# A new order for attention and two feed-forward layers on one core, and the first layer's low words made on ScalarE

## The chip, the cores and the metric

The kernel runs on one core of one Trainium2 chip. The metric is the device time of one execution in microseconds (us). The engines are named as in the profile: PE is TensorE's matmul, PEld its weight load, DVE VectorE, ACT ScalarE, POOL GpSimd, SP SyncE, whose queue issues most DMAs.

## What is computed

Thresholded attention over 4 batches of 8 heads (576 tokens, 64 wide), then two feed-forward layers of 2304 tokens, 512 wide, 2048 hidden. Weights come as 64-bit floats.

```python
scores = scale * np.matmul(q, k.transpose(0, 1, 3, 2))
thresh = np.max(scores, axis=-1, keepdims=True) - tau
scores = np.where(scores >= thresh, scores, -1000000000.0)
scores = scores - np.max(scores, axis=-1, keepdims=True)
attn = np.exp(scores)
attn = attn / (np.sum(attn, axis=-1, keepdims=True) + 1e-09)
x = np.matmul(attn, v)          # then heads side by side: 2304 x 512
...
h = x @ w_in;   g = h * np.cos(h);                      x = g @ w_out      # first layer
h = x @ w_in;   g = s * np.maximum(h, 0.0)**2 + b;      out = g @ w_out    # second layer
```

## The kernel before, in words

**Attention** goes in 16 pairs of heads (`pair(n)`). A pair has nine score tiles of 128 rows by 576; tile 4 is mixed from both heads. For tile i the steps are: `scores` on PE (tile `s`, two PSUM slots in turn), `stat` on DVE (copies `s` to `p` and takes the minimum `mn`), `limit` on POOL (`thr` = `mn` + tau), `expo` on ACT (`e`), `mask` on DVE (compares `p` with `thr`, multiplies by `e`, sums into `sm`). Then `turn` transposes masked tiles on PE (`pt`, four PSUM slots shared with others), `store_turned` copies them to `PT` on ACT, `turn_rest` and `store_rest` do the last columns. `sums` (POOL), `recips` (DVE, tile `r`), `rows` (PE), `spread` (ACT) and `spread2` (SP, by way of DRAM) bring the reciprocals of the row sums to the layout of the output. `weighted(h, k)` multiplies by the values on PE: for each half h five steps k of two matmuls into `av`. `finish` copies `av` to `xs` on ACT, and `normalise` multiplies on POOL into `xT`.

PE's matmuls are of three kinds: `scores`, `turn` and `turn_rest` use 64 rows of the array at a time, `weighted` 64 columns, and the layers all of it. An fp32 matmul of the first two kinds stands as two instructions in the trace (two `weighted` matmuls of a step are x4).

**Layers.** Tokens go in blocks of 512 (one of 256). For each block and each 128 of the hidden width (a step) PE makes `h` by 12 matmuls, DVE, POOL and ACT do the activation, and PE adds 12 matmuls into `acc`. Every operand is a high part rounded to fp32r (`wh`, `xh`, `gh`) and a rest (`wl`, `xl`, `gl`).

**Weights.** `decode` turns one half tile of 64-bit floats (two 32-bit words each, `wr`) into fp32: `magnitude` on ACT, `clamp` on POOL, `shift`, `sign` and `fill` on DVE (`wt`), `high` on POOL or ACT, `low` on POOL. The first 15 half tiles of the first layer (`EARLY`) are decoded beside attention; 17 more after it, and the 32 of the second layer later still.

**The order.** All this is recorded as operations with an engine, a length, a rank and what they need, and `Order.run` draws up the sequence: at each step every engine looks at its first 48 open operations by rank and takes the first that could start. The ranks come from `PLACE`, one number for each kind of operation, plus a base of 12303 for each pair; `SLACK` and `LAG` say how far a later operation may go ahead, and what a hand-over between engines costs. On the chip each engine then executes its own sequence strictly in that order, and waits by semaphores.

Of the kernel before, what the change touches and what calls it, by code (L numbers as in the profile page):

```python
# [10 lines left out]
F32 = mybir.dt.float32  # L11
F32R = mybir.dt.float32r
I32 = mybir.dt.int32
AF = mybir.ActivationFunctionType
ALU = mybir.AluOpType
PSUM = bass.MemoryType.PSUM

P = 128

TINY = 2.0**-15  # L20
HUGE = 3.0e38
TWO_PI = 2.0 * math.pi
# [5 lines left out]
class Order:  # L28
# [6 lines left out]
    SLACK = 0  # L35
    LAG = 90
    WINDOW = 48

# [12 lines left out]
    def add(self, engine, length, rank, fn, after=(), take=(), give=(), tail=0):  # L51
        op = dict(
            n=len(self.ops), engine=engine, length=length, rank=rank, fn=fn,
            after=[a for a in after if a is not None], take=tuple(take), give=tuple(give),
            tail=tail, start=None, end=None,
        )
        self.ops.append(op)
        return op

    def _earliest(self, op, free):  # L60
        t = free
        for a in op["after"]:
# [17 lines left out]
    def run(self):  # L80
# [5 lines left out]
        free = dict.fromkeys(queues, 0.0)  # L86
        done = []
        while any(queues.values()):
# [15 lines left out]
            free[e] = op["end"]  # L104
            for name, _ in op["take"]:
                self.rings[name]["taken"] += 1
            for name, k in op["give"]:
                self.rings[name]["back"][k] = op["end"]
# [7 lines left out]
EARLY = 15  # L116

# [4 lines left out]
    "scores": -3186, "stat": -5231, "exp": -5403, "mask": -12, "turn": 1691, "turned": 1308, "rest": -817,  # L122
    "rested": 530, "sums": -3199, "weigh0": -749, "weigh1": 4124, "weigh_step": 1464, "finish": -3724,
    "normalise": 49805, "keys": -33243, "early": 2.755, "early_step": 0.971, "first": 4.255, "second": 0.531,
    "second_step": 0.992, "first_step": 0.769, "xin": -6179, "active": 7099, "output": 1499,
# [5 lines left out]
def attention_moe_moe2_kernel(  # L131
# [76 lines left out]
    make_identity(nc, ident)  # L208
    ape = actx.enter_context(tc.tile_pool(name="ape", bufs=2))
# [23 lines left out]
    def pair(n):  # L233
# [32 lines left out]
        ks = add("POOL" if n else "ACT", 700, base + PLACE["keys"], scale_keys, after=[lk], take=[tk["ks"]], give=[tk["k"]])  # L266
# [37 lines left out]
        for i in range(9):  # L304
            for _ in range(WEIGH.count(i)):
                yield
            at = base + i * PAIR // 9
# [38 lines left out]
            def mask(i=i):  # L346
                if "sm" not in T:
# [7 lines left out]
            s_ = add("PE", 660 if i == mixed else 620, at + PLACE["scores"], scores, after=[lq, ks] if i == 0 else [], take=[ts],  # L355
                     give=[tk["q"], tk["ks"]] if i == 8 else [], tail=130)
            scored.append(s_)
            m_ = add("DVE", 835, at + PLACE["stat"], stat, after=[s_], take=[tm, tp], give=[ts])
            t_ = add("POOL", 190, at + PLACE["stat"], limit, after=[m_], take=[th])
            e_ = add("ACT", 735, at + PLACE["exp"], expo, after=[m_], take=[te], give=[tm])  # L360
            k_ = add("DVE", 850, at + PLACE["mask"], mask, after=[e_, t_], give=[te, th])
            masks.append(k_)
            if i in (1, 3, 4, 6, 8):
                tiles = [i] if i == mixed else [i - 1, i]
                tt = [ticket("pt"), ticket("pt")]
                r_ = add("PE", 310 * len(tiles), at + PLACE["turn"], lambda t=tiles: turn(t), after=[masks[j] for j in tiles],
                         take=[*tt, *([tk["PT"]] if i == 1 else [])], tail=170)
# [25 lines left out]
        r_ = add("PE", 650, end + PLACE["rest"], turn_rest, after=masks, take=tt, give=ptk, tail=170)  # L393
        for g in range(2):
            c_ = add("ACT", 400, end + PLACE["rested"], lambda g=g: store_rest(g), after=[r_], give=[tt[g]])
# [26 lines left out]
        o1 = add("POOL", 150, end + PLACE["sums"] + 0, sums, after=masks)  # L422
        o2 = add("DVE", 220, end + PLACE["sums"] + 100, recips, after=[o1])
        t1 = ticket("pt")
        o3 = add("PE", 110, end + PLACE["sums"] + 700, rows, after=[o2], take=[t1])
        o4 = add("ACT", 270, end + PLACE["sums"] + 800, spread, after=[o3], give=[t1])
        o5 = add("SP", 150, end + PLACE["sums"] + 900, spread2, after=[o4], take=[tk["rb"]], tail=5000)
# [18 lines left out]
        for h in range(2):  # L446
            yield
            ts = ticket("pt")
            for k in range(5):
                v1 = add(  # L450
                    "PE", 490 + 100 * (k % 4 == 0), end + PLACE[f"weigh{h}"] + k * PLACE["weigh_step"], lambda h=h, k=k: weighted(h, k),
                    after=[*transposed, lv] if h == k == 0 else [v1], take=[ts] if k == 0 else [],
                    give=[tk["PT"], tk["v"]] if h * k == 4 else [],
                    tail=250 * (k == 4),
                )
            f_ = add(
                "ACT", 390, end + PLACE["finish"] + PLACE[f"weigh{h}"], lambda h=h: finish(h), after=[v1, f_],
# [8 lines left out]
        n_ = add("POOL", 1600, end + PLACE["normalise"], normalise, after=[f_, o5], give=[tk["xs"], tk["rb"]])  # L466
# [421 lines left out]
```

## Time and profile before

| what | value |
|---|---|
| median of 3 runs | 1097.76 us (1095.64 to 1100.08) |
| profiled execution | 1095.87 us |
| its span | 1093.3 us |
| mean granted TensorE clock | 0.995 of full speed |
| attention, first score tile to last weighted step | about 5 to 290 us |
| layers | about 274 to 1089 us |

The span runs from the first to the last instruction. The profile below is of the profiled execution; times in rows are us from the span's start unless marked ns.

### The profile page before, as it was taken

The page shows a single profiled execution, that of the slowest core. Times are in us where ns is not written, and L with a number is a line of the kernel's source. Part 1 is how long each engine was busy: PE and PEld are TensorE (multiplying, and loading weights), DVE is VectorE, ACT ScalarE, POOL GpSimd, SP SyncE. Part 2 cuts the span into 40 slices and gives each one's busy share as a digit, 9 for nine tenths or more (in the row PEclk, how much of TensorE's full clock was granted, in tenths as well). Part 3 has the DMA queues.
Part 4 walks back from the last instruction along what each step waited for, and adds up shares of the span by engine and source line. Part 5 has one row for each costly group of instructions (what it writes and reads, how often), then busy time and mean ns, then how long its engine had stood idle before and what let it go on. Part 6 is the DMA issues. An engine that isn't in the chain of part 4 may idle for free.

```text
span 1093.3 us, 17499 instructions
## 1 busy us (share of the span) xinstructions
PE 1051.2 (96%) x6736; PEld 804.5 (74%) x6736; DVE 649.6 (59%) x1206; ACT 491.4 (45%) x880; POOL 497.4 (45%) x556
## 2 busy tenths in 40 slices
PE   6998989899999999999999999999999999999998
PEld 3554555555678788899888888788888898888886
DVE  7998899889899943434534789778511212113111
ACT  6887777878554432323223445444422323223221
POOL 4556465565587643333333776666422222222221
PEclk9999899999999999999999999999999999999999
DMA  4323244242223200000100132323100000001001
GB/s 171 132 89 139 94 133 131 102 134 75 69 97 97 78 20 1 1 1 1 58 1 0 58 97 78 95 79 105 50 1 1 8 32 20 1 1 40 1 1 39
DMA packets 23507, 63.59 MB, mean 58 GB/s; under 512 B 4464, under 2 KB 4736, under 8 KB 23424
## 3 DMA queue, kind: packets, MB, share of 16 engines
q1 hardware_dynamic: 23280, 62.48, 17.7%
q8 instruction: 53, 0.87, 0.3%
q14 instruction: 30, 0.25, 0.1%
q10 hardware_dynamic: 144, 0.00, 0.0%
HBM read 57.67 MB, written 4.79 MB: 57 GB/s over the span
## 4 chain that ended last, share of the span: by engine, by line
PE 84%; DVE 6%; POOL 4%; issue 3%; DMA 1%; ACT 1%; SPq 0%; POOLq 0%; DVEq 0%
PE h L661 36%; PE acc L764 18%; PE acc L762 17%; PE av L434 6%; PE s L318 4%; PE pt L281 2%; DVE p L333 2%; DVE p L350 2%; POOL thr L340 1%; POOL xT L462 1%; DMA wr<-in_w_dram 1%; DVE wt L549 1%; POOL wt L546 1%; POOL wl L189 1%; DVE wt L554 0%
## 5 line engine op out<-in xcount | busy, mean ns | idle before, releaser
L661 PE MATMUL h<-x,wh 128*128 128x512 f32 (+1 forms) x1280 | 369.6, 373 | 4.2 <-DVE r L712 3.5
L189 POOL TENSOR_TENSOR gl<-r,gh 128x512 fp32r<-128x512 f32 x144 | 189.6, 1317 | 334.8 <-DVE gh L735 248.7
L661 PEld LDWEIGHTS h<-x,wh 128*128 128x128 f32 x1280 | 231.2, 188 | 53.9 <-DVE r L712 6.4
L661 PE MATMUL h<-x,wl 128*128 128x512 f32 (+1 forms) x640 | 238.7, 373 | 0.7 <-POOL wl L189 0.7
L691 DVE TENSOR_SCALAR r<-r,s_t,b_t 128x512 f32<-128x512 f32 x72 | 45.8, 636 | 207.9 <-ACT r L226 207.8
L226 ACT ACTIVATE r<-h 128x512 f32<-128x512 f32 x72 | 42.9, 596 | 243.2 <-PE h L661 241.8
L661 PEld LDWEIGHTS h<-x,wl 128*128 128x128 f32 x640 | 120.2, 188 | 23.8 <-POOL wl L189 1.1
L350 DVE SCALAR_TENSOR_TENSOR p<-p,thr,e 128x576 f32<-128x576 f32 x144 | 125.1, 883 | 2.8 <-ACT e L344 2.3
L762 PE MATMUL acc<-gl,wh 128*128 128x512 f32 (+1 forms) x320 | 118.3, 370 | 0.2 <-POOL gl L189 0.2
L344 ACT ACTIVATE e<-p,mn 128x576 f32<-128x576 f32 x144 | 109.8, 771 | 19.3 <-DVE p L350 11.8
L762 PE MATMUL acc<-gh,wl 128*128 128x512 f32 (+1 forms) x320 | 118.0, 369 | 0.0
L762 PE MATMUL acc<-gh,wh 128*128 128x512 f32 (+1 forms) x320 | 118.0, 369 | 0.0
L318 PE MATMUL s<-ks,q 64*128 64x288 f32 x512 | 95.2, 464 | 23.5 <-DVE p L333 17.9
L333 DVE TENSOR_SCALAR_CACHE_REDUCE p<-s 128x576 f32<-128x576 f32 x144 | 106.3, 753 | 17.9 <-PE s L318 16.9
L764 PE MATMUL acc<-wh,gl 128*128 128x512 f32 x288 | 112.6, 391 | 0.0
L764 PE MATMUL acc<-wl,gh 128*128 128x512 f32 x288 | 112.5, 390 | 0.0
L764 PE MATMUL acc<-wh,gh 128*128 128x512 f32 x288 | 112.3, 390 | 0.0
L226 ACT ACTIVATE r<-r,hpi 128x512 f32<-128x512 f32 x72 | 51.9, 721 | 132.7 <-POOL r L704 132.6
L189 POOL TENSOR_TENSOR wl<-wt,wh 128x512 fp32r<-128x512 f32 x64 | 88.0, 1378 | 41.0 <-ACT wh L572 39.8
L340 POOL TENSOR_TENSOR thr<-mn,ptau 128x1 f32<-128x1 f32 x144 | 69.5, 484 | 78.4 <-DVE p L333 77.0
L691 DVE TENSOR_SCALAR r<-h 128x512 int32<-128x512 f32 x72 | 49.6, 689 | 79.2 <-PE h L661 70.8
L434 PE MATMUL av<-PT,v 128*64 128x288 f32 x640 | 93.2, 418 | 0.0
(65 smaller groups left out, 1423.7 us busy)
## 6 DMA issues: line engine op xcount, KB each, us to landing
wr<-in_w_dram SPq DMA_DIRECT2D x64, 512.0 KB, 3.7
q<-in_qt_dram SPq DMA_DIRECT2D x15, 576.0 KB, 3.8
v<-in_va_dram SPq DMA_DIRECT2D x16, 320.0 KB, 3.6
k<-in_kt_dram SPq DMA_DIRECT2D x16, 288.0 KB, 4.0
out_dram<-ob SPq DMA_DIRECT2D x18, 256.0 KB, 2.1
rb<-rd SPq DMA_DIRECT2D x16, 144.0 KB, 3.2
rb<-rd SPq DMA_DIRECT2D x16, 128.0 KB, 3.1
q<-in_qt_dram SPq DMA_DIRECT2D x1, 448.0 KB
```

What stands on the lines that cost most here:

```text
L189: (eng or nc.gpsimd).tensor_tensor(out=o, in0=a, in1=b.bitcast(F32), op=ALU.subtract)
L226: nc.scalar.activation(o, x, fn, **kw)
L318: nc.tensor.matmul(st[:, h, :H2], T["q"][g, c : c + 128], T["ks"][g, hd * H2 : (hd + 1) * H2], start=True, stop=True,)
L333: nc.vector.tensor_scalar(out=T["p", i], in0=T["s", i][:, :, :H2], scalar1=1.0, scalar2=None, op0=ALU.mult, op1=ALU.min, accum_out=T["mn", i],
L340: nc.gpsimd.tensor_tensor(out=T["thr", i], in0=T["mn", i], in1=ptau, op=ALU.add)
L344: nc.scalar.activation(T["e", i], T["p", i], AF.Exp, bias=T["mn", i], scale=-1.0)
L350: nc.vector.scalar_tensor_tensor(out=p, in0=p, scalar=T["thr", i], in1=T["e", i], op0=ALU.is_le, op1=ALU.mult, accum_out=T["sm"][:, i : i ...
L434: nc.tensor.matmul(T["av", h][g, :H2], T["v"][:, hd, k, :], T["PT"][:, 4 if k == 4 else k + 5 * hd, h * H2 : (h + 1) * H2], start=(k == 0) ...
L661: nc.tensor.matmul(B["h"][:, e * n : (e + 1) * n], wt[:, c * P : (c + 1) * P], x, start=(c == 0 and j == 0), stop=(c == HP - 1 and j == 2),)
L691: nc.vector.tensor_scalar(out=o, in0=x, scalar1=s1, scalar2=s2_, op0=ALU.mult, op1=ALU.add)
L762: nc.tensor.matmul(acc[d][:, :n], wt[:, d * P : (d + 1) * P], g, **st)
L764: nc.tensor.matmul(acc[d], g[:, d * P : (d + 1) * P], wt, **st)
```

## The change

The planner gets other lengths for its operations, a `TAIL` for each engine, a hand-over cost on one engine (`SAME`), a `SLACK` of 79 ns in place of 0, and a `port` on which some operations of DVE and POOL exclude each other in the plan. On PE an operation whose kind (`mode`) differs from that before is charged `SWITCH`, and its rank is put back by `STAY`. `PLACE` holds a rank for each tile of a pair, for each step of `weighted`, and for each weight tile, in place of one per kind.

In the first layer `decode` goes another way: `rebased` (ACT) takes the place of `magnitude` and also scales, `cap` (POOL) that of `clamp`; `bits` makes integers of the low words on ACT, in place; on DVE `merge` and `signed` take the place of `shift`, `sign` and `fill`. `high` of the early tiles goes from POOL to ACT. The second layer keeps its way.

```diff
-    SLACK = 0
-    LAG = 90
+    SLACK = 79
+    LAG = 45
+    SAME = 34
+    TAIL = {"PE": 160, "DVE": 83, "ACT": 98, "POOL": 40}
     WINDOW = 48
+    SWITCH = {"rows": 170, "columns": 90, "all": 90}
+    STAY = 41370
...
+        def turns(e, op):
+            return 0 if None in (op["mode"], mode[e]) or op["mode"] == mode[e] else self.SWITCH[op["mode"]]
...
-                    t = self._earliest(op, free[e] if e else 0.0)
+                    t = self._earliest(op, free[e] + turns(e, op) if e else 0.0)
                     if t is not None:
+                        if op["port"]:
+                            t = max(t, port)
...
-                    t, op = next((t, op) for t, op in ready if t <= first + self.SLACK)
+                    t, op = min(
+                        ((t, op) for t, op in ready if t <= first + self.SLACK),
+                        key=lambda x: (x[1]["rank"] + self.STAY * bool(turns(e, x[1])), x[1]["n"]),
+                    )
...
+HIGH = "ACT"
...
-    "normalise": 49805, "keys": -33243, "early": 2.755, "early_step": 0.971, "first": 4.255, "second": 0.531,
...
+    "sums": (-21818, -8534, 18045, 21339, 12855),
+    "weigh": (33675, 21168, 2835, -5114, 19447, 28585, 17682, 28408, -1599, 40340),
...
+        def rebased():
+            T["t"] = wtp.tile([P, 512], I32, tag="wt", name=f"wt{nm}")
+            nc.scalar.activation(T["t"].bitcast(F32), T["raw"][:, :, 1].bitcast(F32), AF.Abs, scale=2.0**-112)
+
+        def cap():
+            tf = T["t"].bitcast(F32)
+            nc.gpsimd.tensor_scalar(out=tf, in0=tf, scalar1=CAP, scalar2=0.0, op0=ALU.min, op1=ALU.max)
...
+        def bits(scale):
+            def fn():
+                low = T["raw"][:, :, 0]
+                nc.scalar.activation(low, low.bitcast(U32), AF.Copy, scale=scale)
+            return fn
...
+        def merge():
+            nc.vector.scalar_tensor_tensor(
+                out=T["t"], in0=T["t"], scalar=3, in1=T["raw"][:, :, 0], op0=ALU.logical_shift_left, op1=ALU.bitwise_or
+            )
+
+        def signed():
+            nc.vector.scalar_tensor_tensor(
+                out=T["t"], in0=T["raw"][:, :, 1], scalar=-0x80000000, in1=T["t"], op0=ALU.bitwise_and, op1=ALU.bitwise_or
+            )
```

What this does to the sequences shows at three places; names hold pair and tile (`s12_7` is score tile 7 of pair 12).

On PE, in the middle of pair 12, before: the steps of pair 11's second half (`av11_1`) between score tiles (the transposes of `turn` that stand between these rows are left out).

```order
L434 MATMUL av11_0_3560<-PT11_3252,v11_3125 64x288 x10
...
L434 MATMUL av11_1_3605<-PT11_3252,v11_3125 64x288 x4
L318 MATMUL s12_7_3615<-ks12_3099,q12_3097 128x288 x2
L434 MATMUL av11_1_3605<-PT11_3252,v11_3125 64x288 x2
...
L318 MATMUL s12_8_3643<-ks12_3099,q12_3097 128x288 x2
L434 MATMUL av11_1_3605<-PT11_3252,v11_3125 64x288 x2
L318 MATMUL s13_0_3659<-ks13_3377,q13_3375 128x288 x2
```

The same place of the change.

```order
L370 MATMUL s12_5_3535<-ks12_3077,q12_3074 128x288 x2
L485 MATMUL av11_0_3542<-PT11_3233,v11_3124 64x288 x10
L370 MATMUL s12_6_3580<-ks12_3077,q12_3074 128x288 x2
L370 MATMUL s12_7_3588<-ks12_3077,q12_3074 128x288 x2
...
L370 MATMUL s12_8_3620<-ks12_3077,q12_3074 128x288 x2
L370 MATMUL s13_0_3627<-ks13_3364,q13_3353 128x288 x2
L485 MATMUL av11_1_3635<-PT11_3233,v11_3124 64x288 x10
```

Both halves are now ten matmuls in a row; score tiles 7 and 8 moved ahead of the second half. Groups of weighted matmuls that stand together fall from 69 to 32 over the whole program.

On DVE, at the end of pair 12, before: masks (L350), the reciprocal (L403), stats (L333).

```order
L350 SCALAR_TENSOR_TENSOR p12_8_3663,sm12_3457<-p12_8_3663,thr12_8_3674,e12_8_3676 128x576
L350 SCALAR_TENSOR_TENSOR p13_0_3672,sm13_3735<-p13_0_3672,thr13_0_3685,e13_0_3714 128x576
L403 RECIPROCAL r12_3776<-sm12_3457 128x9
L350 SCALAR_TENSOR_TENSOR p13_1_3712,sm13_3735<-p13_1_3712,thr13_1_3723,e13_1_3756 128x576
L333 TENSOR_SCALAR p13_3_3783,mn13_3_3782<-s13_3_3719 128x576
```

The same place of the change: masks are L402, stats L385, the reciprocal L454, `merge` L649, `signed` L654.

```order
L402 SCALAR_TENSOR_TENSOR p12_8_3647,sm12_3474<-p12_8_3647,thr12_8_3657,e12_8_3661 128x576
L649 SCALAR_TENSOR_TENSOR wt0_6_0_3595<-wt0_6_0_3595,wr0_6_0_3262 128x512
L385 TENSOR_SCALAR p13_1_3718,mn13_1_3717<-s13_1_3684 128x576
L454 RECIPROCAL r12_3740<-sm12_3474 128x9
L385 TENSOR_SCALAR p13_2_3743,mn13_2_3742<-s13_2_3713 128x576
L402 SCALAR_TENSOR_TENSOR p13_0_3653,sm13_3752<-p13_0_3653,thr13_0_3666,e13_0_3687 128x576
L402 SCALAR_TENSOR_TENSOR p13_1_3718,sm13_3752<-p13_1_3718,thr13_1_3750,e13_1_3748 128x576
L385 TENSOR_SCALAR p13_3_3786,mn13_3_3785<-s13_3_3745 128x576
L654 SCALAR_TENSOR_TENSOR wt0_6_0_3595<-wr0_6_0_3262,wt0_6_0_3595 128x512
```

A weight pass and a stat stand between the last mask of the pair and the reciprocal; the two weight passes stand apart, one at the end of a pair and one after the stat of tile 3.

On ACT, in pair 12, the change: exponentials (L396), the copy of the weighted sum (L494), `rebased` (L630), `bits` (L642) and `high` (L623).

```order
L396 ACTIVATE e12_4_3562<-p12_4_3551,mn12_4_3550 128x576
L623 ACTIVATE wh0_4_1_3575<-wt0_4_1_3317 128x512
L494 ACTIVATE xs11_3583<-av11_0_3542 128x288
L396 ACTIVATE e12_5_3586<-p12_5_3558,mn12_5_3557 128x576
L630 ACTIVATE wt0_6_0_3595<-wr0_6_0_3262 128x512
...
L642 ACTIVATE wr0_6_0_3262<-wr0_6_0_3262 128x512
L396 ACTIVATE e12_8_3661<-p12_8_3647,mn12_8_3646 128x576
L494 ACTIVATE xs11_3583<-av11_1_3635 128x288
L396 ACTIVATE e13_0_3687<-p13_0_3653,mn13_0_3652 128x576
```

Before, one pass of decoding (`magnitude`) stood in each pair on ACT; now there are three, each between exponentials.

## Rows read from the trace of the kernel before

**Rows 1.** The page: busy time, share of the span and instructions of each engine.
```profile
PE 1051.2 (96%) x6736; PEld 804.5 (74%) x6736; DVE 649.6 (59%) x1206; ACT 491.4 (45%) x880; POOL 497.4 (45%) x556
```
**Rows 2.** Windows by stage: busy time of each engine, clock, DMA share, GB/s.
```profile
23.10:278.60 255.50, 229.69 (x2806) 132.52 (x2802) 231.68 (x594) 202.24 (x410) 144.27 (x218) 0.98 0.34 110
...
300.00:400.00 100.00, 97.46 (x416) 77.29 (x415) 84.50 (x103) 44.25 (x71) 68.92 (x66) 1.00 0.26 79
400.00:690.00 290.00, 289.97 (x1443) 244.31 (x1442) 163.25 (x226) 101.38 (x162) 132.06 (x136) 1.00 0.10 30
```
**Rows 3.** The reciprocals: count, shortest, median, longest (ns), first and last start.
```profile
L403 DVE RECIPROCAL r<-sm x16: 200/215/217, 23.1 to 278.6; 128x9 f32<-128x9 f32 x16
```
**Rows 4.** Windows of one pair without and one with weight decoding; columns as above.
```profile
40.20:53.96 13.76, 13.37 (x147) 8.06 (x147) 12.52 (x37) 11.50 (x25) 7.27 (x12) 1.00 0.35 110
211.80:228.88 17.08, 15.10 (x187) 8.58 (x187) 15.26 (x41) 13.65 (x28) 9.48 (x15) 1.00 0.36 121
```
**Rows 5.** Waits of DVE from 23.1 to 278.6: us in total, times, longest.
```profile
DVE p L333 <- PE s L318: 14.5, 33, 1.0
DVE r L403 <- POOL sm L399: 4.5, 6, 0.9
```
**Rows 6.** Timeline of DVE: start, duration, instruction, idle before it and releaser.
```profile
204.24 1.27 DVE L350 SCALAR_TENSOR_TENSOR p<-p,thr,e 128x576 f32<-128x576 f32 x1
...
207.19 0.81 DVE L350 SCALAR_TENSOR_TENSOR p<-p,thr,e 128x576 f32<-128x576 f32 x1
...
207.93 0.75 DVE L333 TENSOR_SCALAR_CACHE_REDUCE p<-s 128x576 f32<-128x576 f32 x1
...
208.61 0.75 DVE L333 TENSOR_SCALAR_CACHE_REDUCE p<-s 128x576 f32<-128x576 f32 x1
...
211.80 0.22 DVE L403 RECIPROCAL r<-sm 128x9 f32<-128x9 f32 x1 [0.94 <-POOL sm L399]
...
220.64 0.76 DVE L333 TENSOR_SCALAR_CACHE_REDUCE p<-s 128x576 f32<-128x576 f32 x1 [0.49 <-PE s L318]
```
**Rows 7.** Timeline of PE in pair 12, from score tile 5 on.
```profile
213.43 0.76 PE L318 MATMUL s<-ks,q 64*128 64x288 f32 x4 [1.99 <-DVE p L333]
...
214.32 0.76 PE L318 MATMUL s<-ks,q 64*128 64x288 f32 x4
...
215.50 2.65 PE L434 MATMUL av<-PT,v 128*64 128x288 f32 x20
218.08 0.71 PE L281 MATMUL pt<-ident,p 64*128 64x64 f32 x16
218.72 1.19 PE L434 MATMUL av<-PT,v 128*64 128x288 f32 x8
219.84 0.76 PE L318 MATMUL s<-ks,q 64*128 64x288 f32 x4
220.52 0.71 PE L434 MATMUL av<-PT,v 128*64 128x288 f32 x4
221.16 0.46 PE L281 MATMUL pt<-ident,p 64*128 64x64 f32 x8
```
**Rows 8.** Groups by line up to 285: count, busy, mean ns, idle before.
```profile
L350 DVE SCALAR_TENSOR_TENSOR p<-p,thr,e 128x576 f32<-128x576 f32 x144 | 125.1, 883 | 2.8 <-ACT e L344 2.3 <-POOL thr L340 0.3
...
L189 POOL TENSOR_TENSOR wl<-wt,wh 128x512 fp32r<-128x512 f32 x15 | 20.8, 1388 | 1.1
...
L554 DVE SCALAR_TENSOR_TENSOR wt<-wr,wt 128x512 int32<-128x512 int32 x16 | 11.4, 713 | 0.4
...
L542 ACT ACTIVATE wt<-wr 128x512 f32<-128x512 f32 x16 | 10.8, 674 | 6.6 <-DMA wr<-in_w_dram 6.6
...
L549 DVE TENSOR_SCALAR wt<-wt 128x512 int32<-128x512 int32 x16 | 7.2, 450 | 0.0
```
**Rows 9.** Waits of PE from 290 to the end.
```profile
PE h L661 <- DVE r L712: 3.5, 4, 1.0
PE h L661 <- POOL wl L189: 0.7, 1, 0.7
```
**Rows 10.** Group of the shift from 300 to 400.
```profile
L549 DVE TENSOR_SCALAR wt<-wt 128x512 int32<-128x512 int32 x14 | 12.8, 914 | 0.0
```

More of the change, by code (lines that the diff above doesn't have):

```diff
@@ L116 @@
 EARLY = 15
+EARLY_WAY = "act"
+LATE_WAY = "act"
+HIGH = "ACT"
 WEIGH = (3, 4)
@@ L392, in pair @@
         tt = [ticket("pt"), ticket("pt")]
-        r_ = add("PE", 650, end + PLACE["rest"], turn_rest, after=masks, take=tt, give=ptk, tail=170)
+        r_ = add("PE", 600, base + PLACE["rest"], turn_rest, after=masks, take=tt, give=ptk, mode="rows")
         for g in range(2):
-            c_ = add("ACT", 400, end + PLACE["rested"], lambda g=g: store_rest(g), after=[r_], give=[tt[g]])
+            c_ = add("ACT", 265, base + PLACE["rested"], lambda g=g: store_rest(g), after=[r_], give=[tt[g]])
             transposed.append(c_)
@@ L575, in low @@
             psub(W[half][1], T["t"].bitcast(F32), W[half][0])
-        early = opened is None
-        o = add("SP", 60, rank - 6000, load, take=[tr], tail=4000)
-        o = add("ACT", 675, rank, magnitude, after=[o], take=[tt])
-        o = add("POOL", 620 if early else 720, rank, clamp, after=[o])
-        o = add("DVE", 430 if early else 900, rank, shift, after=[o])
-        o = add("DVE", 690 if early else 1100, rank, sign, after=[o])
-        o = add("DVE", 690 if early else 1150, rank, fill, after=[o], give=[tr])
@@ L584, in decode @@
-        o = add("POOL" if early else "ACT", 630, rank, high, after=[o, opened], take=[tw])
-        o = add("POOL", 1270 if early else 1370, rank, low, after=[o], give=[tt])
+        def rebased():
[4 more added lines that the diff above has]
+            nc.gpsimd.tensor_scalar(out=tf, in0=tf, scalar1=CAP, scalar2=0.0, op0=ALU.min, op1=ALU.max)
@@ new lines, in signed @@
+        def signed():
+            nc.vector.scalar_tensor_tensor(
+                out=T["t"], in0=T["raw"][:, :, 1], scalar=-0x80000000, in1=T["t"], op0=ALU.bitwise_and, op1=ALU.bitwise_or
+            )
+        early = opened is None
+        way = EARLY_WAY if early else LATE_WAY if layer == 0 else "dve"
+        l = add("SP", 60, rank - 6000, load, take=[tr], tail=4000)
+        o = add("ACT", 580, rank, magnitude if way == "dve" else rebased, after=[l], take=[tt])
+        if way != "dve":
+            l = add("ACT", 580, rank, bits(LOWEST if way == "act" else 2.0**-29), after=[l])
@@ L586, in decode @@
+        o = add("POOL" if early and HIGH == "POOL" else "ACT", 740 if early and HIGH == "POOL" else 540, rank, high, after=[o, opened], take=[tw])
+        o = add("POOL", 1300 if early else 1270, rank, low, after=[o], give=[tt], port=early)
         split_op[half] = o
@@ L638, in low @@
                 psub(xtile[c][1][:, :n], xT[:, c, a:b], xtile[c][0][:, :n], nc.vector)
-            o = add("ACT", 200 + n * 0.83, rank, high, after=[*need, ox], take=[xt[c]])
-            splits.append(add("DVE", 160 + n * 1.7, rank, low, after=[o]))
+            o = add("ACT", 110 + n * 0.81, rank, high, after=[*need, ox], take=[xt[c]])
+            splits.append(add("DVE", 80 + n * 1.15, rank, low, after=[o]))
         gs = {}
@@ L808, in store @@
                 nc.sync.dma_start(out=out[a + d * P : a + (d + 1) * P, :], in_=B["ob"])
-            c_ = add("ACT" if d % 2 else "DVE", 650, rank, copy, after=[o], take=tks)
+            c_ = add("ACT" if d % 2 else "DVE", 600, rank, copy, after=[o], take=tks)
             copies.append(c_)
```

134 lines of the change are left out of this document (92 added, 42 removed).

## Prediction

> **What bounds the kernel now.** I read the page's busy line first [rows 1]: TensorE (PE) is busy for 96% of the span, so the question is where those 96% are work and where they only look it. The windows by stage [rows 2] answer that. From 300 us on, PE is full: in the stretch from 400 to 690 it is busy for 289.97 of 290.00 us. The change leaves the number of these matmuls as it is, so nothing but their holes can be won there. Between the first and the last reciprocal, 23.1 to 278.6 us [rows 3], it is another matter: PE is busy 229.69 and VectorE (DVE) 231.68 of 255.50 us. Neither is full, and fifteen head pairs pass in that time, 255.5 / 15 = 17.03 us each.
>
> Two pairs show what a period is made of [rows 4]. One without weight decoding took 13.76 us with DVE busy for 12.52; one with it took 17.08 with DVE busy for 15.26, ACT for 13.65 and PE for 15.10. DVE has the most work, but idles 1.82 us in that period. What it idles for stands in the waits [rows 5]: over the stretch 14.5 us for score tiles and 4.5 us for the row sums. Both are seen in this pair [rows 6]: the reciprocal waits 0.94 us, and a stat, the pass that copies a score tile and takes its minimum, waits 0.49 us.
>
> The PE rows tell why [rows 7]. PE first stands still for 1.99 us because the score tile's PSUM slot is not yet free (DVE is behind). Then it runs ten weighted steps, a transpose and four more steps in a row, and the next score tile starts at 219.84, 5.52 us after the last one at 214.32. Now DVE has nothing to do. So each engine stalls the other in turn; neither is the bound alone, their order is.
>
> **DVE work.** Each early weight tile has three DVE passes now: the shift, 0.450 us on the mean, and two passes of two inputs each, 0.71 [rows 8]. The change keeps two passes of two inputs over the same tiles and drops the shift. 15 x 0.450 = 6.8 us, taken from 231.68, leaves 224.9 us. That the two new passes cost what the old two did follows from the shapes, and their sum is the same; if each cost as much as a mask (0.883, more elements), 15 x 2 x 0.17 = 5 us would come back.
>
> **DVE idle time**, 255.50 - 231.68 = 23.8 us. Two moves aim at it. The reciprocal now stands behind a weight pass and a stat (0.71 + 0.75 us of cover), and its row sums are ahead of the normalising product on GpSimd; that is more than the 0.94 waited. On PE all ten steps of a half stand together, with two score tiles right ahead of the second run and one ahead of the first. I walked the tightest place: from the end of the stat of tile 3 DVE has a weight pass, mask 2, stats 4 and 5, and masks 3 and 4 before it needs tile 6. By the distance of starts that follow each other (mask 0.74 from 207.19 to 207.93, stat 0.68 from 207.93 to 208.61 [rows 6]; the weight pass 0.71) that is 0.71 + 3 x 0.74 + 2 x 0.68 = 4.29 us. PE meanwhile does tile 5 (0.68 from 219.84 until the next kind starts [rows 7]), ten steps (2.58 from 215.50 to 218.08) and tile 6 until its stat starts (0.80, from 219.84 to 220.64 [rows 6, 7]): 4.06 us, plus a hand-over. So DVE is just covered, and jitter will show. The bounds are 0 and 23.8; I leave 3 us, near the lower end, since both named waits have cover but one with a margin of only about 0.2 us. The stretch becomes 224.9 + 3 = 228 us, a gain of 27.5; with the bounds 30.6 and 6.8.
>
> **PE switches.** Today the second half's ten steps are cut up: one step alone takes 0.64 us (220.52 to 221.16), ten in a row 2.58, or 0.52 each [rows 7]. Weighted pieces fall from 69 to 32. That is 37 x 0.12 = 4.4 us of PE over the stretch. It is not added: PE is not the engine with the most work, and what it saves makes its 4.06 us shorter than DVE's 4.29. If this cover were gone, by steps of 0.64 (ten of them 6.4), DVE would wait 3.6 us there in each pair.
>
> **ACT** gets the low words (one pass more) and the rounded copy that GpSimd made. Neither pass is in the trace in that form; the nearest is ACT's pass over the same strided words, 0.674 us [rows 8], and I bound one by nothing (hidden) and twice that. 13.65 + 2 x 0.674 = 15.0 us per pair, as much as DVE has (224.9 / 15). I take it as hidden, since neither result is needed by the scores of the same pair, and put the danger into a rival; if the cover is gone, 2 x 0.674 x 15 = 20 us would show. GpSimd loses the copy and is busy 144.27 of 255.50 us [rows 2]: nothing.
>
> **Entry into the feed-forward part.** After 290 us PE waits 3.5 us for DVE's sine stages and 0.7 for GpSimd's low parts [rows 9]; in the stretch from 300 to 400 DVE is at 84.5 of 100 us [rows 2], of which the shift alone takes 12.8 us [rows 10], and this goes. Stages stand less long behind decoding. I take 3.5 us off, between 0 and 4.6 (all four waits). The loads move on SP's queue: the weight load stands ahead of the row-sum store of the same pair now. It waits for a raw buffer that the second weight pass frees right after the stat of tile 3; the store behind it needs a copy that ACT makes only after the exponential of tile 3, so the store would wait about as long by itself: 0, at the worst a normalising product that comes late, for which GpSimd's idle 111 us leave room.
>
> **Start**, 23.1 us: the first pair's order is nearly the same; 0, within 1 us either way. The granted clock is 0.98 over the stretch [rows 2], a short time at the lower of its two levels; PE was waited for too little for that to count, 0.
>
> **Sum.** 27.5 + 3.5 = 31.0 us. The profiled execution took 1095.87 (span 1093.3 and 2.6 around it), so it becomes 1064.9. The median of the runs is 1.9 above it, 1097.76; from there 1066.8, say 1067.
>
> **Rivals.**
> The idle time only moves. The walk shows a margin of 0.2 us in one place, and another wait of 1.5 us per pair, behind PSUM banks or an exponential, would restore the 23.8 us. For it: ACT, PE and DVE would all be at 14 to 15 us per period, and such lines run with gaps. Against: in the pair without decoding DVE idled 1.24 us, not 1.82, on the old order. Then only 6.8 + 3 us are won: 1088. Chance 0.14.
>
> Shared access of DVE and GpSimd. A mask took 1.27 us instead of 0.81 [rows 6] while GpSimd was at a product; the masks' mean of 0.883 [rows 8] holds some 10 us of this (144 x 0.07). In the new order the low-part subtraction (1.388 us [rows 8]) follows the limit of tile 5, just where masks 3 and 4 run, and the normalising product follows the last masks. If each costs one mask 0.45 us more than today, 15 x 0.9 = 13.5 us are lost again: 1080. It decides from one collision per pair more. Chance 0.13. The Trainium skill (GPSIMD Engine Reference, Key points) says that GpSimd shares its SBUF interfaces with VectorE and contends with instructions that have two SBUF inputs; both new weight passes are such, and by that rule every GpSimd product beside them or a mask pays. The trace agrees as to masks; the stats, which read PSUM, take 0.75 and 0.76 in these rows.
>
> ACT becomes the bound, and the kernel is slower. In ACT's queue the copy out of the weighted sum stands right behind ten steps of 2.58 us, twice a pair, with the exponential of the next tile behind it. If ACT has no work left at three quarters of both, it needs 15.0 + 3.87 = 18.9 us per pair; 15 x (18.9 - 17.03) = 28, less 3.5: 1122. The turn lies at 2 us of such idling per pair (15.0 + 2.0 = 17.03). For it: exponentials are queued behind those copies. Against: the weighted run waits for nothing that stands behind it on ACT, and ACT's order puts a rounded copy and an exponential ahead. Chance 0.05.
>
> **Chances and range.** The forecast holds 0.66, idle time 0.14, contention 0.13, ACT 0.05; 0.02 is left for something unseen that makes no difference. Runs of before spread by 0.4%, so 0.5% (5.5 us) is about what can be told from no change. Faster: the first three, 0.93, less 0.02 for a stretch in which two of them meet: 0.91. Same 0.04, slower 0.05. Low end: no idle time (30.6), all PE waits (4.6), and half of the masks' 10 us: 1097.8 - 40 = 1058, with the start's 1 us and the spread of runs 1055. High end: the idle case at 1088 cut in the middle of its share, 1086. This leaves out some 0.07 + 0.05 above and 0.06 below.
>
> **What would show it.** Right: reciprocals from about 23 to 251 us; no reciprocal waits on sums; DVE over 96% busy between; 32 weighted groups; PE's waits for DVE near 10 us instead of 21; fewer PE holes from 300 to 400. Wrong: a period above 16.5 us, or masks whose mean is over 0.95, or ACT without a gap while DVE waits for exponentials. Weight passes longer than 0.9 us each would break the DVE term.

## The result and the profile after

The changed kernel takes 1058.78 us (median of 4 runs, 1058.31 to 1059.02) against 1097.16 for the kernel before (4 runs, 1095.64 to 1100.08): a ratio of 0.9647, 95% interval 0.9626 to 0.9668. The forecast was 1067, with a range from 1055 to 1086. The profiled execution took 1058.82 us, its span is 1057.0, and the granted clock is 1.00 throughout.

The page of the changed kernel, busy time of each engine, answers to [rows 1]:

```profile
PE 1038.1 (98%) x6736; PEld 805.0 (76%) x6736; DVE 612.1 (58%) x1175; ACT 504.1 (48%) x927; POOL 496.3 (47%) x541
```

Windows of the changed kernel, columns as in [rows 2]: from the first reciprocal to the last, 100 us of the layers, and all that follows the last reciprocal.

```profile
22.30:239.50 217.20, 216.02 (x2767) 132.33 (x2766) 215.93 (x580) 209.50 (x436) 137.71 (x205) 1.00 0.42 131
...
264.00:364.00 100.00, 97.57 (x418) 77.50 (x417) 71.67 (x90) 49.12 (x84) 70.40 (x66) 1.00 0.28 85
...
239.50:1057.00 817.50, 807.98 (x3813) 664.11 (x3811) 380.65 (x550) 280.55 (x469) 349.75 (x317) 1.00 0.12 38
```

The same last part in the kernel before, and 3.4 us of its attention at a low clock:

```profile
278.60:1093.30 814.70, 806.26 (x3808) 663.57 (x3799) 401.75 (x567) 274.83 (x448) 343.62 (x317) 1.00 0.12 38
...
125.10:128.50 3.40, 2.67 (x11) 1.38 (x13) 3.19 (x9) 2.33 (x6) 1.54 (x4) 0.50 0.00 0
```

The reciprocals of the changed kernel, which answer to [rows 3]:

```profile
L454 DVE RECIPROCAL r<-sm x16: 199/205/215, 22.3 to 239.5; 128x9 f32<-128x9 f32 x16
```

The profiled execution became 37.05 us shorter, in four parts: the start 0.8 (23.1 to 22.3); the stretch between the reciprocals 38.3 (255.5 to 217.2, a period of 14.48 us in place of 17.03); after the last reciprocal 2.8 **longer** (814.7 to 817.5); outside the span 0.75 shorter (1095.87 - 1093.3 = 2.57, now 1.82). In the stretch DVE's work fell from 231.68 to 215.93 us and its idle time from 23.8 to 1.3.

The waits of DVE over the stretch answer to [rows 5]; only this row is left:

```profile
DVE p L402 <- ACT e L396: 0.2, 1, 0.2
```

And those of PE in the same stretch. Before, it waited there for DVE's stats, 21.4 us in two rows:

```profile
PE s L318 <- DVE p L333: 16.5, 15, 2.0
PE s L325 <- DVE p L333: 4.9, 5, 1.7
```

Now these are all:

```profile
PE s L377 <- DVE p L385: 0.4, 1, 0.4
PE pt L334 <- ACT xs L494: 0.3, 1, 0.3
```

PE in the middle of a pair, its timeline in the changed kernel, answers to [rows 7]:

```profile
183.33 0.98 PE L334 MATMUL pt<-ident,p 64*128 64x64 f32 x16
184.29 0.76 PE L370 MATMUL s<-ks,q 64*128 64x288 f32 x4
184.98 2.65 PE L485 MATMUL av<-PT,v 128*64 128x288 f32 x20
187.56 1.24 PE L370 MATMUL s<-ks,q 64*128 64x288 f32 x8
188.63 0.66 PE L334 MATMUL pt<-ident,p 64*128 64x64 f32 x16
189.18 1.48 PE L370 MATMUL s<-ks,q 64*128 64x288 f32 x8
190.59 2.65 PE L485 MATMUL av<-PT,v 128*64 128x288 f32 x20
```

Both halves of the weighted product are one piece of 2.65 us, and two score tiles (x8) stand ahead of the second. DVE's timeline in the same pair, answering to [rows 6]:

```profile
184.16 0.69 DVE L654 SCALAR_TENSOR_TENSOR wt<-wr,wt 128x512 int32<-128x512 int32 x1
...
187.59 0.81 DVE L402 SCALAR_TENSOR_TENSOR p<-p,thr,e 128x576 f32<-128x576 f32 x1
...
188.36 0.76 DVE L385 TENSOR_SCALAR_CACHE_REDUCE p<-s 128x576 f32<-128x576 f32 x1
...
189.72 0.81 DVE L402 SCALAR_TENSOR_TENSOR p<-p,thr,e 128x576 f32<-128x576 f32 x1
...
190.46 1.15 DVE L402 SCALAR_TENSOR_TENSOR p<-p,thr,e 128x576 f32<-128x576 f32 x1
...
193.64 0.81 DVE L402 SCALAR_TENSOR_TENSOR p<-p,thr,e 128x576 f32<-128x576 f32 x1
...
194.38 0.68 DVE L649 SCALAR_TENSOR_TENSOR wt<-wt,wr 128x512 int32<-128x512 int32 x1
194.99 0.74 DVE L385 TENSOR_SCALAR_CACHE_REDUCE p<-s 128x576 f32<-128x576 f32 x1
195.66 0.20 DVE L454 RECIPROCAL r<-sm 128x9 f32<-128x9 f32 x1
```

The last mask, a weight pass, a stat and the reciprocal follow without a gap: no bracket stands behind a row. GpSimd beside them has its subtraction and its `cap`:

```profile
187.73 1.82 POOL L240 TENSOR_TENSOR wl<-wt,wh 128x512 fp32r<-128x512 f32 x1
...
189.79 1.22 POOL L634 TENSOR_SCALAR wt<-wt 128x512 f32<-128x512 f32 x1
```

In the kernel before, this is what GpSimd did when the mask of 1.27 us at 204.24 [rows 6] started:

```profile
203.62 1.27 POOL L189 TENSOR_TENSOR wl<-wt,wh 128x512 fp32r<-128x512 f32 x1
```

Where DVE's 15.8 us of work went shows in the groups over the stretch, first of the kernel before:

```profile
L350 DVE SCALAR_TENSOR_TENSOR p<-p,thr,e 128x576 f32<-128x576 f32 x134 | 117.1, 888 | 2.8 <-ACT e L344 2.3 <-POOL thr L340 0.3
...
L189 POOL TENSOR_TENSOR wl<-wt,wh 128x512 fp32r<-128x512 f32 x14 | 19.5, 1396 | 1.0
...
L549 DVE TENSOR_SCALAR wt<-wt 128x512 int32<-128x512 int32 x14 | 5.7, 409 | 0.0
```

and of the changed kernel:

```profile
L402 DVE SCALAR_TENSOR_TENSOR p<-p,thr,e 128x576 f32<-128x576 f32 x134 | 110.1, 844 | 1.2 <-ACT e L396 0.2
...
L240 POOL TENSOR_TENSOR wl<-wt,wh 128x512 fp32r<-128x512 f32 x13 | 23.7, 1822 | 0.9 <-ACT wh L623 0.8
...
L649 DVE SCALAR_TENSOR_TENSOR wt<-wt,wr 128x512 int32<-128x512 int32 x15 | 11.5, 764 | 0.0
...
L654 DVE SCALAR_TENSOR_TENSOR wt<-wr,wt 128x512 int32<-128x512 int32 x14 | 9.6, 688 | 0.0
```

The masks are 7.0 us shorter, the shift's 5.7 are gone, and 1.9 us of splitting `x` have left the stretch (2.6 us there before, 0.7 now). GpSimd's subtraction has become longer, 1.40 to 1.82 us on the mean.

### The profile page after: what moved, and what is told of

Its sections match the earlier page's. It is cut to its first block, busy times and chain, and to the rows that moved or that the text cites. A ratio compares the mean times of both kernels' runs of the same rounds, so it can differ in the third digit from the quotient of the medians.

```text
span 1057.0 us, 17568 instructions
## 1 busy us (share of the span) xinstructions
PE 1038.1 (98%) x6736; PEld 805.0 (76%) x6736; DVE 612.1 (58%) x1175; ACT 504.1 (48%) x927; POOL 496.3 (47%) x541
## 4 chain that ended last, share of the span: by engine, by line
PE 88%; DVE 5%; ACT 3%; POOL 2%; issue 1%; DMA 1%; DVEq 0%; POOLq 0%; ACTq 0%
PE h L753 34%; PE acc L859 19%; PE acc L857 15%; PE av L485 7%; PE s L370 7%; PE pt L334 4%; DVE x L240 1%; PE ptr L433 1%; DMA wr<-in_w_dram 1%; PE s L377 1%; POOL r L796 1%; ACT e L396 1%; DVE r L804 1%; DVE wt L649 1%; DVE p L402 1%
## 5 line engine op out<-in xcount | busy, mean ns | idle before, releaser
L240 POOL TENSOR_TENSOR gl<-r,gh 128x512 fp32r<-128x512 f32 x144 | 193.5, 1344 | 326.5 <-DVE gh L827 252.9
L753 PEld LDWEIGHTS h<-x,wl 128*128 128x128 f32 x640 | 120.2, 188 | 22.5
L402 DVE SCALAR_TENSOR_TENSOR p<-p,thr,e 128x576 f32<-128x576 f32 x144 | 118.1, 842 | 1.2 <-ACT e L396 0.2
L396 ACT ACTIVATE e<-p,mn 128x576 f32<-128x576 f32 x144 | 111.8, 778 | 10.0 <-DVE p L385 6.4
L240 POOL TENSOR_TENSOR wl<-wt,wh 128x512 fp32r<-128x512 f32 x64 | 96.0, 1503 | 20.7 <-ACT wh L623 20.1
L385 DVE TENSOR_SCALAR_CACHE_REDUCE p<-s 128x576 f32<-128x576 f32 x144 | 104.1, 745 | 2.4 <-PE s L370 2.4
L392 POOL TENSOR_TENSOR thr<-mn,ptau 128x1 f32<-128x1 f32 x144 | 64.0, 449 | 75.6 <-DVE p L385 73.6
L370 PE MATMUL s<-ks,q 64*128 64x288 f32 x512 | 91.9, 446 | 7.5 <-ACT ks L314 5.5
L796 POOL TENSOR_SCALAR r<-r 128x512 f32<-128x512 f32 x72 | 50.1, 696 | 101.4 <-DVE r L793 99.7
```

The costliest lines, as they stand in the source:

```text
L240: (eng or nc.gpsimd).tensor_tensor(out=o, in0=a, in1=b.bitcast(F32), op=ALU.subtract)
L370: nc.tensor.matmul(st[:, h, :H2], T["q"][g, c : c + 128], T["ks"][g, hd * H2 : (hd + 1) * H2], start=True, stop=True,)
L385: nc.vector.tensor_scalar(out=T["p", i], in0=T["s", i][:, :, :H2], scalar1=1.0, scalar2=None, op0=ALU.mult, op1=ALU.min, accum_out=T["mn", i],
L392: nc.gpsimd.tensor_tensor(out=T["thr", i], in0=T["mn", i], in1=ptau, op=ALU.add)
L396: nc.scalar.activation(T["e", i], T["p", i], AF.Exp, bias=T["mn", i], scale=-1.0)
L402: nc.vector.scalar_tensor_tensor(out=p, in0=p, scalar=T["thr", i], in1=T["e", i], op0=ALU.is_le, op1=ALU.mult, accum_out=T["sm"][:, i : i ...
```

## The experiments

Diffs are against the changed kernel unless said otherwise. Its runs spread by 0.1% and those of the kernel before by 0.4%, and the times of variants are compared with 1058.78 directly. The changed kernel was run in one series only, and the median of the kernel before was 1095.16 to 1097.16 us in the four series, so a difference of less than 2 us means little.

**1 and 2. The new order with the old passes**, first for all tiles of the first layer, then only for the 17 decoded after attention. In the first, the old passes take the places of the new ones in the sequence.

```diff
+        if layer == 0 and True:         # in the second: if layer == 0 and not early:
+            rebased, bits, cap = magnitude, lambda s: lambda: None, clamp
+
+            def merge():
+                shift()
+                sign()
+
+            signed = fill
```

> The changed kernel with its sequence kept, but the first layer's weights decoded by the old passes at the same places: shift and sign together where merge stands, fill where signed stands, no pass on the low words; the rounded copy stays on ScalarE. Theory (the order took the waits away, and VectorE's work is now what a pair takes): 15 shifts of 0.45 us come back in attention, ScalarE's relief does not count: 1059 + 7 = 1066, period 14.9 instead of 14.5. Rival (the decoding was the gain, ScalarE's words above all): more than half of the 38 us goes, 1080 or more. Second rival (TensorE sets the period): no change within 2 us.

> As the run with the old passes, but for the 17 late weight tiles of the first layer alone. Theory (the holes at the entry into the layers are waits for a chain over several engines and the weight DMA, not VectorE's load): within 2 us of the changed kernel, 1057 to 1061. Rival (VectorE's load was the bound there, so the dropped shift did pay and something else ate it): 17 x 0.9 = 15 us more work on VectorE, 4 us or more later, 1063 and up.

Measured: 1071.77 us (1070.97 to 1072.09; ratio 0.9780, 0.9741 to 0.9819) and 1066.79 (1066.64 to 1067.65; ratio 0.9739, 0.9700 to 0.9777). Of the 13.0 us between the first and the changed kernel, 5.0 belong to the early tiles and 8.0 to the late ones: the first run's stretch is 4.2 us longer than that of the changed kernel, its start 0.7, and the part behind the last reciprocal 8.1 (825.6 against 817.5). The first run's theory named 7 us, all of it in attention; 4.2 came there, and it had left out the late tiles. The window of the first between its reciprocals shows DVE as full as in the changed kernel, only with more to do, 220.67 of 221.40 us:

```profile
23.00:244.40 221.40, 217.71 (x2773) 133.84 (x2769) 220.67 (x594) 204.97 (x421) 139.39 (x207) 1.00 0.41 128
```

The waits of PE in the second, from its last reciprocal to 400 us, are 9.2 us together in five rows, the first two of them these:

```profile
PE h L761 <- DVE r L812: 5.9, 6, 1.7
PE h L761 <- DVE x L240: 1.8, 3, 1.1
```

In the changed kernel the same waits, from its last reciprocal to 400 us, are 3.8:

```profile
PE h L753 <- DVE r L804: 2.5, 3, 0.9
PE h L753 <- DVE x L240: 1.3, 3, 0.6
```

So the theory that the late passes matter little fell: DVE's load does count at the entry into the layers, and 5.4 of the 8.0 us stand in these two views.

**3. The old order with the new passes**: the kernel before with the first layer's new `decode` and `high` on ACT, its planner and `PLACE` as they were (diff against the kernel before).

```diff
+        if layer == 0:
+            l = add("SP", 60, rank - 6000, load, take=[tr], tail=4000)
+            o = add("ACT", 675, rank, rebased, after=[l], take=[tt])
+            l = add("ACT", 675, rank, bits, after=[l])
...
+            o = add("DVE", 690 if early else 1100, rank, merge, after=[o, l])
+            o = add("DVE", 690 if early else 1150, rank, signed, after=[o], give=[tr])
+            o = add("ACT", 630, rank, high, after=[o, opened], take=[tw])
```

> The kernel before, with its numbers and planner, but the first layer decoded the new way and the rounded copy on ScalarE. Theory (order is the gain): the two stalls of each pair stay, only the shift goes: 0 to 7 us below before, 1090 to 1097. Rival (decoding is the gain): 1075 or below. Third way: ScalarE's two more passes, put in by an order that was not drawn for them, make it slower, 1098 to 1105.

Measured: 1094.47 us (9 runs, 1091.22 to 1097.29), ratio 0.9991 (0.9970 to 1.0011): nothing. Its window and DVE's waits between the reciprocals say where the saved work went.

```profile
22.90:277.40 254.50, 228.10 (x2787) 132.26 (x2785) 225.32 (x581) 216.73 (x440) 124.19 (x207) 0.99 0.34 113
```

```profile
DVE p L338 <- PE s L323: 21.4, 35, 1.5
DVE r L408 <- POOL sm L404: 3.2, 7, 0.8
```

DVE has 6.4 us less to do (231.68 to 225.32), and waits 6.9 us longer for score tiles (14.5 [rows 5] to 21.4). Where the order bounds, a lighter engine only waits longer. Behind its last reciprocal this run takes 815.3 us (277.4 to 1092.7), the kernel before 814.7.

**4. No charge for changes of kind**, the sequence drawn again with the same `PLACE`.

```diff
-    SWITCH = {"rows": 170, "columns": 90, "all": 90}
-    STAY = 41370
+    SWITCH = {"rows": 0, "columns": 0, "all": 0}
+    STAY = 0
```

> The changed kernel with the charge for a change of kind on TensorE at zero (SWITCH and STAY 0), the order drawn anew by the planner with all else kept: 75 groups of weighted steps instead of 32. Theory (TensorE is nearly full in attention, so cutting costs what it costs): 43 groups x 0.12 to 0.25 us = 5 to 11 us, 1064 to 1070, and VectorE idles for score tiles again. Rival (TensorE's switches are hidden): 1059 to 1061.

Measured: 1105.36 us (1102.92 to 1110.73), ratio 1.0101 (1.0066 to 1.0137): some 1% above the kernel before, as neither theory had it. Between its reciprocals DVE and PE wait above all as follows (a window of the stretch, 255.90 us, has DVE busy for 230.10 and a granted clock of 0.97):

```profile
DVE p L385 <- PE s L370: 9.8, 15, 2.1
DVE p L402 <- ACT e L396: 8.8, 20, 2.2
```

```profile
PE pt L334 <- ACT PT L441: 9.0, 11, 1.2
PE pt L334 <- ACT PT L353: 7.6, 9, 1.8
```

PE now waits for ACT's copies, 16.6 us in these two rows; in the changed kernel it doesn't. The run doesn't price the cuts, since everything moved; run 9 prices two of them in one place.

**5 to 8. One pass more on each engine**, sequence unchanged: the same work done twice for each early tile (for score tile 1 of pairs 1 to 15 on PE).

```diff
+            if opened is None:                              # 5, VectorE: signed once more
+                nc.vector.scalar_tensor_tensor(...)
...
+            for _ in range(2 if opened is None else 1):     # 6, ScalarE: rebased twice
...
-                for h in range(2):                          # 7, TensorE
+                for h in (0, 1, 0, 1) if n and i == 1 else (0, 1):
...
+            for _ in range(2 if opened is None else 1):     # 8, GpSimd: cap twice
```

> The changed kernel, sequence kept, with the last VectorE pass of each of the 15 early weight tiles done twice (same result; 0.61 us from start to start). Theory (VectorE's work is what a pair takes): all of it shows, 15 x 0.61 = 9 us, 1068. Rival (TensorE or ScalarE sets the period): 0 to 4 us, 1059 to 1063.

> The same for ScalarE: the scaling pass of each early weight tile done twice (0.58 us). Theory (VectorE): ScalarE has about 0.5 us idle per pair, 0 to 3 us, 1059 to 1062. Rival (the three engines are tied in one ring): 15 x 0.58 = 8.7 us, 1067.

> The same for TensorE: the matmuls of score tile 1 of 15 pairs done twice into the same place (0.54 us). Theory (VectorE): TensorE looks full (216.0 of 217.2 us) but part of it is matmuls whose ends overlap a wait; 14.1 us of work per pair against 14.5: 0 to 4 us, 1059 to 1063. Rival (TensorE is the bound): 15 x 0.54 = 8 us, 1067.

> The same for GpSimd: the cap of each early weight tile done twice (0.6 to 1.0 us). Theory (VectorE): GpSimd has 5 us idle per pair, 0 to 1 us, 1059 to 1060. Rival (GpSimd's passes take VectorE's access to SBUF): the passes beside it are stretched, 15 x 0.3 = 4 us or more, 1063 and up.

Measured, with the work added in the stretch: by how much later the engine's next instruction starts, over the 14 or 15 doubled pieces that stand there. Score tile 1, for one, holds PE for 0.54 us in the changed kernel (the next start is at 194.07) and, doubled, for 1.03 (the next start is at 195.95); first the changed kernel, then run 7:

```profile
193.53 0.71 PE L370 MATMUL s<-ks,q 64*128 64x288 f32 x4
```

```profile
194.92 1.20 PE L370 MATMUL s<-ks,q 64*128 64x288 f32 x8
```

| doubled on | added, us | time, us | against 1058.78 |
|---|---|---|---|
| VectorE | 10.2 | 1068.94 (1068.34 to 1069.42) | +10.2 |
| ScalarE | 10.8 | 1062.17 (1062.13 to 1062.18) | +3.4 |
| TensorE | 6.8 | 1060.31 (1059.67 to 1061.19) | +1.5 |
| GpSimd | about 14 | 1060.23 (1060.14 to 1060.24) | +1.5 |

Two of their windows between the reciprocals, VectorE's first:

```profile
22.10:249.00 226.90, 217.42 (x2764) 131.93 (x2763) 225.17 (x594) 209.49 (x437) 137.96 (x207) 1.00 0.40 125
```

TensorE's:

```profile
22.20:241.00 218.80, 217.22 (x2819) 136.18 (x2816) 217.27 (x579) 210.61 (x434) 137.91 (x206) 1.00 0.41 130
```

The theory, that DVE's work sets the period, came out in all four, on ScalarE at the edge of its range. Only on VectorE is all of the added work paid. On ScalarE about a third is, where DVE then waits for exponentials:

```profile
DVE p L402 <- ACT e L396: 4.4, 14, 0.3
```

TensorE's run is the one to look at twice: PE stood at 216.02 of 217.20 us already, took in 6.8 us more, and its busy time grew by 1.2. Part of its busy time had been waiting that the records count as work. It shows in its rows above: 16 transposes take 0.98 us at 183.33 and 0.66 at 188.63.

**9. The second half cut again**: everything as in the changed kernel, but two steps of the second half stand ahead of score tile 8, and one ahead of the next pair's tile 0 (60 weighted groups in place of 32).

```diff
+    def ahead(op, of):
+        todo.remove(op)
+        todo.insert(todo.index(of), op)
+
+    for n in range(1, NPAIR - 1):
+        for k in (0, 1):
+            ahead(at["w", n - 1, 1, k], at["s", n, 8])
+        ahead(at["w", n - 1, 1, 2], at["s", n + 1, 0])
```

> The changed kernel with one thing moved back on TensorE in 14 pairs: the second half's ten steps stand cut as 4, 2 and 4 matmuls with score tiles 8 and 0 between them, as the kernel before had them, all else in its sequence. Theory (two score tiles ahead of an uncut run keep VectorE fed): score tile 8 comes 1.1 us later in each pair while VectorE has only two masks to do, and two cuts cost 0.2 us each; 14 x 0.5 to 0.9 us = 7 to 13 us, 1066 to 1072, with VectorE waiting for score tiles again. Rival (VectorE's stock of work covers it): below 3 us, 1059 to 1062.

Measured: 1063.68 us (1063.65 to 1063.79), 4.9 more, below the theory and above its rival. DVE waits for score tiles again, once in each of the 14 pairs, 0.34 us on the mean:

```profile
DVE p L385 <- PE s L370: 4.7, 14, 1.1
```

4.7 of the 4.9 us stand in this row. So the uncut second half, with two score tiles ahead of it, is cover that DVE needs. The place that the forecast walked is another one, the first half between tiles 5 and 6, and it stays whole here.

**10. No decoding after attention.** The 17 late half tiles take the weights of early ones.

```diff
-            decode((0, *half), PLACE["first"][j], orest)
+            def same(f=f, part=part):
+                W[0, f, part] = W[0, (7, 6)[part], part]
+            split_op[0, f, part] = add(None, 0, 0, same, after=[orest, split_op[0, (7, 6)[part], part]], take=[tw])
```

> The changed kernel without decoding the first layer's 17 late weight tiles (it leaves them out and uses an early tile's weights in their place). Theory (the holes of some 10 us at the entry come from the late decoding, through GpSimd's and ScalarE's queues): most of them go, 1050 to 1053. Rival (they are the activation's own latency over four engines): 1057 to 1059.

Measured: 1067.17 us (1067.06 to 1067.91), 8.4 more with less work, a miss for both theories. The planner drew the entry anew. PE's waits from the last reciprocal to 400 us are 4.2 us in place of 3.8, the last three periods became longer too (47.1 us together in place of 43.8), and nothing follows for the cause at the entry.

**11 and 12. Two other ways to share the work**, both of which the changed code offers: GpSimd adds the low words in place of ScalarE and VectorE, and two tiles fewer are decoded beside attention. Both redraw the sequence.

```diff
-EARLY_WAY = "act"
+EARLY_WAY = "pool"      # in 11
-EARLY = 15
+EARLY = 13              # in 12
```

> The changed kernel with EARLY_WAY pool: for the 15 early weight tiles GpSimd multiplies by eight and adds the low words, VectorE has one pass left; the planner draws the order anew. Theory (VectorE's work sets the period): 15 x 0.61 = 9 us less, 1050, if nothing new stops it. Rival (GpSimd's 2.3 us more per pair run beside masks and stretch them, and the order is not drawn for it): 1060 to 1075.

> The changed kernel with EARLY 13 instead of 15: two weight tiles less beside attention, two more at the entry; the planner draws the order anew. Theory (VectorE is the bound in attention and not after it): 2 x 1.3 us gained in attention, lost again in part at the entry, 1056 to 1060. Rival (the late decoding is what makes TensorE's holes there): each late tile costs more than its 1.3 us, 1061 to 1066.

Measured: 1095.91 us (9 runs, 1093.34 to 1096.77; ratio 0.9985, 0.9964 to 1.0007) and 1077.21 (1076.28 to 1077.41). Each is slower than both of its theories had it. The first is back at the time of before: DVE waits 8.9 us for score tiles and 5.4 for exponentials between its reciprocals, and its masks take 887 ns on the mean.

In the second the stretch is 218.3 us (22.5 to 240.8). The edit did not take the two tiles out of it: 15 `merge` and 14 `signed` passes stand there as in the changed kernel, with one rounded copy less (13 for 14), so the gain that the theory named was not put to the test. Nearly all of the 18.4 us is lost behind the last reciprocal (834.6 us against 817.5). No variant beat the changed kernel.

## Why the prediction was right, and where it was not

**What bounds.** Right: neither PE nor DVE bounded attention before, the order did. Run 3 shows it from one side (lighter passes in the old order: 0.7 us less, within the spread), run 1 from the other (the new order with the old passes: 1095.21 to 1071.77, 23.4 us less); the rounded copy is on ACT in both. Together they give more than their sum, 36 to 38 us, because the order makes DVE the bound and only then do lighter passes on DVE pay. What each part of the new order gives is open: run 9 cuts one of the two halves again (4.9 us), no run takes away the reciprocal's cover alone, and run 4 moved everything.

**DVE idle time.** Forecast 23.8 to 3, measured 1.3. Both named waits are gone, and the walk of the tightest place held, with less room than it named. PE takes 4.07 us there (from tile 5 at 184.29 to the stat of tile 6 at 188.36, forecast 4.06). DVE takes 4.17 (from its weight pass at 184.16 until mask 4, started at 187.59, gives way at 188.33, forecast 4.29), and starts 0.13 us before PE; so the stat of tile 6 waits 0.03 us, and nothing of the 0.2 us of cover is left.

**DVE work** is the term that was mis-sized: 6.8 us less were forecast, 15.8 came. The shift gave 5.7, with 14 passes in the stretch. The new passes cost 1.7 us more than the two old ones (11.5 + 9.6 against 9.7 + 9.7), inside the bound of 5: there is one `merge` more in the stretch, and one of 1.92 us (at 237.47, beside a normalising product); the others take the 0.68 to 0.69 us of the old two, as forecast. The unforeseen gain is the masks, 7.0 us. The low end of the range had half of their 10 us; the sum had none. The splitting of `x` adds 1.9 by leaving the stretch and the stats 1.3 (97.3 to 96.0). The 1.6 that are left stand in no group, since the records of an engine overlap and its groups add up to more than its busy time.

The masks gained because fewer of them meet a long pass of GpSimd. Before, 18 of the 134 took over 0.95 us, 10.2 us more together than at 0.81 each: nine started while GpSimd was at a normalising product (6.0 us of it), five at the subtraction (2.8), three at the rounded copy (1.1), one at `clamp`. Now 13 are long, by 4.0 us, and twelve of them started beside `cap`. So the copy's move to ACT is worth some 1 us. The rest goes with the order: with the copy on ACT the masks' mean is 845 ns in run 1, which has the old passes, and 857 in run 3, but 889 in run 4.

**The contention rival** did not come, for its place was wrong. Masks are stretched less than before (one of 1.15 us in this pair), and it is GpSimd that became slower beside DVE, its subtraction 1.82 us in place of 1.40. That was nearly free: doubling a GpSimd pass costs 1.5 us for about 14. The rows show which of two passes pays: the one that starts second. Before, the mask at 204.24 started behind the subtraction at 203.62 (which is what GpSimd was at there, not a product) and took 1.27 us for 0.81. Now the subtraction at 187.73 starts behind a mask (187.59), and so does `cap` at 189.79 (189.72), and both are long, 1.82 and 1.22; the mask at 190.46 starts behind `cap` and takes 1.15. The Trainium skill (GPSIMD Engine Reference, Key points) has GpSimd contend over shared SBUF interfaces with DVE instructions that have two SBUF inputs. The trace agrees, with the 1.15 us mask and the 1.82 us subtraction, and here it was mostly the one with time to spare that paid.

**ACT** as hidden: right, and near its edge. ACT is busy for 209.50 of 217.20 us, 14.0 us a pair for the forecast 15.0, and another 10.8 us cost 3.4 (run 6). The third rival, ACT as bound, did not come.

**PE switches** at nothing: right, since 6.8 us more of PE cost 1.5 (run 7). But groups matter by where they stand (run 9). The forecast's 3.6 us, for the cover gone, is miscounted: a step is two matmuls, and both are in the row of 0.64 us (x4), so a half has five such steps, not ten. Five make 3.2 us, PE's part 4.68 and DVE's wait 0.39 in a pair. No run cuts that half; run 9's two cuts in the other one cost 0.34.

Of the signs that the forecast named, the reciprocals end earlier (239.5 for 251), none waits on sums, DVE is busy for 99% of the stretch, and PE waits 0.4 us for DVE where 10 were expected. One hardly came: fewer holes on PE in the 100 us after the entry, 97.57 busy against 97.46 [rows 2].

**Entry into the layers**: this step failed. The forecast took 3.5 us off; the part behind the last reciprocal is 2.8 longer. PE's busy time in it grew by 1.7 (806.26 to 807.98), of which three layer matmuls are some 0.7 (nine started ahead of the last reciprocal before, six now, 0.23 us each), and its idle time by 1.1 (8.44 to 9.52). The forecast let PE's waits go with the shift's load on DVE. In the old order they only change their place: in run 3 PE's wait for DVE's sine stages falls from 3.5 to 1.7 us, its waits for other passes, GpSimd's above all, rise from 1.1 to 3.9, and the part takes as long as before (815.3 us). In the new order the lighter passes do pay, 8.0 us (run 2), more than the bound of 4.6, and DVE's load in the 100 us shown went from 84.5 to 71.7. What was left out is that the new order costs more there: with the old late passes it is slower than the old order by some 11 us behind the last reciprocal (2.8 + 8.0). Why it costs that is open; run 10 was to tell and did not.

**Clock** at 0 was slightly off: before, 10 us of the stretch ran at the lower level (the 0.50 window above is in it), and in the changed kernel no such time is left. The periods don't show its price: the three that hold it (from 124.2 us on) took 17.80, 18.15 and 17.47 us, but the two ahead of them, at the full clock, 18.14 and 17.80. The runs of the kernel before show it better: the seven whose mean granted clock is 1.00 took 1092.46 to 1094.08 us, the four at 0.99 or just below 1099.47 to 1104.07. So the profiled execution, at 0.995, is some 2 to 3 us longer than one without that time, and of the 38.4 us between the medians some 4 go with the clock.

The sum by measured terms: 15.8 of work and 22.5 of idle time in the stretch, 0.8 at the start, 0.75 outside, less 2.8 behind, are 37.05, against 31.0 forecast. For the 0.75 no run shows a cause. That the total came so near is in part luck: DVE's work gave 9.0 us more than forecast, the entry 6.3 less.

## What to carry to other kernels

When two engines stand at 90% and wait for each other in turn, first walk the order of one period and find which wait lacks cover; lighter work gives nothing until that is mended (run 3), and afterwards all work on the engine that then bounds shows in the time (runs 1 and 5). Which engine that is, is better found by doubling a small pass on each than by the busy column: PE at 99% took 6.8 us more for 1.5. Where a mask and a pass of GpSimd met here, the later starter became longer, so the order of starts chooses who pays. Numbers that draw a sequence hold for the operations that they were drawn for: runs 4, 11 and 12 changed one setting each and lost 18 to 47 us.

## What the runs showed of the hardware

In run 12 PE stood still for 3.15 us and then ran at the lower of its two levels, 1.2 GHz, for about 3.4 us. The timeline of PE in that run, and the windows before and behind its start:

```profile
283.61 0.39 PE L857 MATMUL acc<-gh,wl 128*128 128x512 f32 x1
287.15 0.73 PE L753 MATMUL h<-x,wh 128*128 128x512 f32 x2 [3.15 <-DVE r L804]
```

```profile
284.00:287.50 3.50, 0.35 (x2) 0.32 (x3) 1.89 (x4) 2.96 (x6) 2.62 (x4) 1.00 0.39 129
287.50:291.00 3.50, 3.50 (x10) 2.75 (x9) 3.08 (x4) 2.19 (x5) 3.30 (x3) 0.54 0.27 90
```

The ten matmuls of that window start about 0.43 us apart, and those ahead of the pause 0.23, so by an estimate from these starts the wait of 3.15 us cost about 10 x 0.20 = 2 us more behind it. That the clock shows 0.54 only after the pause, when PE is busy again, is worth knowing when one reads such windows.
